# Small float32 matmuls of an attention stage moved into 64x32 and 128x32 tiles of TensorE, in a fused attention and two-MLP kernel

## The chip, the cores and the metric

The kernel is one program on one core of a Trainium2 chip. TensorE (PE in the rows; PEld is its weight loading, which runs beside the matmuls), VectorE (DVE), ScalarE (ACT) and SyncE (SP) take part; GpSimd only builds an identity matrix at the start. SP issues all DMAs. The metric is the device time of one execution in microseconds (us); the kernel before took 736.26 us, the median of three runs from 735.78 to 737.3.

## The reference

For each of 4 batches b and 8 heads h, tokens x[b,h] (512 x 64) and states st[b,h] (32 x 64) attend to each other, and two MLPs follow on all 4 x 544 rows:

```python
scores = scale * x @ state.T                 # 512 x 32 for each (b, h)
a = softmax(scores, over the 32 states)
xread = a @ state                            # 512 x 64
scores2 = scale * state @ x.T                # 32 x 512: the same products, transposed
a2 = softmax(scores2, over the 512 tokens)
sread = a2 @ x                               # 32 x 64
x = concat([xread, sread], axis=2)           # heads side by side: 2176 rows of 512
x = softplus(x @ w_in) @ w_out               # first MLP, d_ff 2048
h = x @ w_in2
out = (max(h, 0) + alpha * min(h, 0)) @ w_out2
```

All arrays are float32. The MLP products are made of three passes over "hi" and "lo" parts in a reduced float32 format; the scores and the states' read are plain float32 matmuls.

## The kernel before, in words

The weights arrive as 64-bit words that hold float32 numbers in another encoding; `decode` (L319) loads a chunk of 128 x 512 into a staging buffer and takes two ACT and two DVE operations to turn it into floats, and `split` (L252) makes the hi part on ACT and the lo part on DVE.

Attention of one batch has five parts. `scores` (L434) is called for two halves k of the 512 tokens. Each half is 8 matmuls whose stationary operand is a 128 x 128 block of x and whose moving operand is 64 columns of the states, zero-padded so that two heads share the 128 rows; the result stands with tokens in the partitions and (head, state) in the columns. ACT copies it to SBUF (L449), and DVE and ACT make the softmax over the 32 states of each head (L450 to L457). `columns` (L460) transposes that result for the first MLP. `rows` (L472) transposes the copied scores on TensorE (L478), so that (head, state) stands in the partitions, and takes the softmax over 512 tokens (L487 to L492). `back` (L502) transposes it again (L510). `read` (L515) multiplies: for each of 4 head pairs and 4 token blocks a 128 x 128 block of x is stationary and 64 columns of the softmax move (L523).

The first MLP uses that xread is a product too: instead of multiplying xread with w_in, `heads_of_m` (L543) multiplies the states with w_in head by head, in two row tiles of 64 partitions that lie side by side (L550), ACT copies the result to `tf` (L556), and `make_m` (L558) brings the four pieces of a batch together by DMA into `mf` and splits them into `m`. The first of these, for batch 0 and the first quarter of the columns, is made on TensorE by `make_first_m` (L573) with full 128 x 128 blocks of padded states (L580). A unit of the first MLP, `step1` (L612), is 6 matmuls `ph<-at,m`, a softplus on ACT (L586), a split into `gs`, and 12 matmuls `pa<-gs,wo` two units later. There are 64 units, 16 for each batch. The banks `ph` are two, so a unit can't begin before the softplus of the unit two before it has read its bank.

The order on each engine is set by a planner. A string (PROGRAM, L1064) lists the steps; each adds operations with engine, cost and dependencies to a graph (`G.add`), and `order` (L111) lists them by due time with a model of the engines. Where it sees TensorE idle near the start it puts in filler matmuls (L1056), each a 128 x 128 matmul on the identity, which write a bank that nobody reads. Each engine then runs its list strictly in that order, and SP issues its DMAs in order too.

The exponential and the softplus live in two different tables of ACT, and each change between them is an ACT_TABLE_LOAD.

Of the kernel before, what the change touches and what calls it, by code (L numbers as in the profile page):

```python
# [22 lines left out]
P = 128  # L23
# [10 lines left out]
NST = 2  # L34
# [39 lines left out]
class Graph:  # L74
# [36 lines left out]
    def order(self):  # L111
# [29 lines left out]
        while placed < n:  # L141
# [31 lines left out]
            if delay:  # L173
                busy = max(busy, t + LAND) + delay - LAND
                delay = busy - t - c
# [20 lines left out]
def attention_then_mlps_kernel(ctx: ExitStack, tc: tile.TileContext, xT, xn, st, st0, w1i, w1o, w2i, w2o, alpha, out):  # L196
# [31 lines left out]
    SB = [lambda b=b: part("sbb", None, F32, 1024)[:, b * 512:(b + 1) * 512] for b in range(2)]  # L228
    WO = [[part(f"wo{j}_{i}", None, F32R) for j in range(2)] for i in range(2)]
    STG = [part(f"st{i}", None, I64, 512) for i in range(NST)]  # L230
# [40 lines left out]
    def load(dst, src, w, r=(), nbytes=0):  # L271
        G.add(SP, 0.06, lambda: nc.sync.dma_start(out=now(dst), in_=now(src)), r, w, delay=LAND + nbytes / RATE)
# [39 lines left out]
    def stg(i):  # L312
        return STG[i] if i < NST else part("sbb", "stg2", I64, 512)

    def third_stage():
        G.add(SP, 0.0, lambda: None, [], [("sb", 0), ("sb", 1)] + [("st", NST, k) for k in range(4)])
        stages[1] = NST + 1

# [66 lines left out]
    def load_state(pair):  # L385
        load(stf, st[pair], [("xf", B)], nbytes=P * 2048)

    def state_of(b):
        return SB[b]().rearrange("p (c f) -> p c f", c=KC) if b < 2 else stf

    def load_first(b):
        load(lambda: SB[b]().rearrange("p (c f) -> p c f", c=KC), st0[b], [("sb", b)], nbytes=P * 2048)

# [12 lines left out]
    def attention(b):  # L406
# [4 lines left out]
        ssb = sz_t[:, :1024].rearrange("p (k c) -> p k c", k=4)  # L411
# [22 lines left out]
        def scores(k):  # L434
            p, pk = bank()
            p_s = p.rearrange("p (q c) -> p q c", q=2)

            def mm():
                for q in range(2):
                    for hp in range(4):  # L440
                        pos, half = hp ^ (b % 2), (hp ^ b) % 2
# [5 lines left out]
            sa, za = [szk[0]] if k == 0 else [szk[1]], [szk[2]] if k == 0 else [szk[3]]  # L447
            G.add(PE, 16 * NARROW, mm, xtk[2 * k:2 * k + 2] + [("sb", b) if b < 2 else ("xf", B)], [pk], load=0.24)
            G.add(ACT, act_us(512, True), lambda: A.activation(ssb[:, sk, :], p_s, AF.Copy), [pk], sa)  # L449
# [22 lines left out]
        def rows():  # L472
            ps = [bank() for _ in range(2)]

            def mm():
                for hg in range(2):
                    for blk in range(4):
                        T.transpose(ps[hg][0][:, blk * P:(blk + 1) * P], ssb[:, blk, hg * P:(hg + 1) * P], ident)  # L478

            G.add(PE, 0.88, mm, szk[:2], [ps[0][1], ps[1][1]], load=0.49)  # L480
            for hg in range(2):
                c = slice(hg, hg + 1)
                p, pk = ps[hg]
                nk, sk, ek = smk(("n", hg)), smk(("s", hg)), [szk[hg]]

                def chain(c=c, p=p, hg=hg):
                    return [lambda: V.tensor_reduce(out=nb[:, c], in_=p, axis=AX.X, op=ALU.max),  # L487
                            lambda: V.tensor_scalar(out=nb[:, c], in0=nb[:, c], scalar1=-SCALE, scalar2=None, op0=ALU.mult),
                            lambda: A.activation(e2[:, hg, :], p, AF.Exp, bias=nb[:, c], scale=SCALE, accum_out=s2[:, c]),
                            lambda: V.tensor_scalar(out=s2[:, c], in0=s2[:, c], scalar1=1e-9, scalar2=None, op0=ALU.add),  # L490
                            lambda: V.reciprocal(out=s2[:, c], in_=s2[:, c]),
                            lambda: V.tensor_scalar(out=e2[:, hg, :], in0=e2[:, hg, :], scalar1=s2[:, c], scalar2=None, op0=ALU.mult)]  # L492

                f = chain()
                G.add(DVE, dve_us(512), f[0], [pk], nk)
                G.add(DVE, 0.07, f[1], [], nk)
                G.add(ACT, 0.66, f[2], nk + [pk], ek + sk, table="exp")
                G.add(DVE, 0.07, f[3], [], sk)
                G.add(DVE, 0.07, f[4], [], sk)
                G.add(DVE, 0.4, f[5], sk, ek)  # L500
# [14 lines left out]
        def read():  # L515
            p, pk = bank(False)
            p_r = p[:, :256].rearrange("p (c f) -> p c f", c=KC)

            def mm():
                for hp in range(4):  # L520
# [5 lines left out]
            G.add(PE, 32 * NARROW, mm, xsk + szk[2:], [pk], load=0.24)  # L526
            cs = slice(b * NS, (b + 1) * NS)
            for j in range(2):
                pr = slice(64 * j, 64 * j + 64)
                half = j ^ (b >> 1)  # L530
                split(srt[pr, 0, :, cs], srt[pr, 1, :, cs], p_r[pr, :, half * NS:(half + 1) * NS], 128, [pk], [("sr", b, j)], psum=True)

        return {"l": lambda: (load_x(0), load_x(1), load_s()), "i": lambda: load_x(0), "j": lambda: load_x(1), "k": load_s,
                "s": lambda: (scores(0), scores(1)), "c": columns, "r": rows, "b": back, "x": read}
# [8 lines left out]
    def heads_of_m(g, c):  # L543
# [9 lines left out]
        for e in range(2):  # L553
            k = 2 * (c % 2) + e
            dst = TF[:, (4 * (c // 2) + k) * 512:(4 * (c // 2) + k + 1) * 512]
            G.add(ACT, act_us(512, True), lambda dst=dst, i=banks[e]: A.activation(dst, PX[i], AF.Copy), [("px", banks[e])], [("tf", c // 2, k)])  # L556

    def make_m(b, g):  # L558
# [5 lines left out]
        tf = TF.rearrange("p (h k f) -> p h k f", h=2, k=4)  # L564
        for q in range(4):
            k = q ^ (2 * (b & 1) + (b >> 1))
            r = slice(32 * q, 32 * q + 32)
            load(mf[r], tf[r, :, k, :], [("mf", i, hg, q) for hg in range(2)], [("tf", hg, k) for hg in range(2)], nbytes=32 * 4096)
# [4 lines left out]
    def make_first_m():  # L573
        s = mslot[0, 0] = ring("m", NM)
        for hg in range(2):
            i = ring("ph", 2)
            p, pk = PH[i], ("ph", i)
            for k in range(2):
                c = 2 * hg + k
                G.add(PE, 0.86, lambda p=p, c=c, k=k: T.matmul(p, state_of(0)[:, c, :], wf(c), start=k == 0, stop=k == 1),  # L580
                      [("sb", 0), ("wi", 1, c, "hi")], [pk])
            split(lambda hg=hg: m_ap(s)[:, 0, hg, :], lambda hg=hg: m_ap(s)[:, 1, hg, :], p, 512, [pk], [("m", s, hg, 0), ("m", s, hg, 1)], psum=True)
# [125 lines left out]
    XS = [("wi0_0", wik(0, 0)), ("wi1_0", wik(0, 1)), ("wo0_0", wok(0, 0)), ("wo1_0", wok(0, 1)), ("at0", atk(0)), ("tf", [("tf", hg, k) for hg in range(2) for k in range(4)]),  # L708
# [390 lines left out]
```

## Time and profile before

| | |
|---|---|
| median of 3 runs | 736.26 us (735.78 to 737.3) |
| profiled execution, own time | 736.82 us |
| its span, first to last instruction | 734.9 us |
| mean granted clock of TensorE | 0.995 of full |
| PE, PEld, DVE, ACT busy | 98%, 84%, 68%, 60% of the span |

A time in a row is counted from the start of the span. "a<-b" means that the instruction writes a and reads b. A plain float32 matmul leaves two records (x counts) for each instruction, and a transpose, or a matmul in the reduced format, one.

### The profile page before, as it was taken

To read this page: it belongs to the slowest core of one execution; us is meant where nothing else is said; L and a number is where in the kernel's file an instruction comes from. 1 tells how busy PE (TensorE), PEld (TensorE's weight loads), DVE (VectorE), ACT (ScalarE), POOL (GpSimd) and SP (SyncE) were. 2 spreads that over 40 slices of the span, in tenths; PEclk is the share of its full clock that TensorE was granted. 3 is DMA by queue.
4 is the path that set the end of the run, shared out by engine and by line. 5 is a ranking of instruction groups with operands and counts; after the bars stand their busy time and mean duration, and the time that the engine had idled before them with its cause. 6 is when DMAs were issued, how large, how long until landed. Compare 5 with 4: busy or idle time off the path is not lost.

```text
span 734.9 us, 10324 instructions
## 1 busy us (share of the span) xinstructions
PE 722.5 (98%) x3644; PEld 616.5 (84%) x3644; DVE 496.1 (68%) x935; ACT 438.9 (60%) x863; POOL 0.7 (0%) x6
## 2 busy tenths in 40 slices
PE   9998999999999999999999999999999999999996
PEld 8967887887788778888899988898898988888884
DVE  5978883776688678777889757954655664555452
ACT  5888986886776676776467545533444543443341
POOL 0000000000000000000000000000000000000000
PEclk9999999999999999999999999999999999999998
DMA  8559355574657588586569955455755454675632
GB/s 287 217 174 249 97 182 143 161 211 148 208 174 230 168 253 221 178 283 233 158 220 316 337 191 194 157 181 207 254 192 187 169 197 177 237 276 175 243 115 72
DMA packets 51224, 148.28 MB, mean 202 GB/s; under 512 B 7140, under 2 KB 21732, under 8 KB 44516
## 3 DMA queue, kind: packets, MB, share of 16 engines
q1 hardware_dynamic: 51172, 147.62, 61.0%
q8 instruction: 29, 0.48, 0.3%
q14 instruction: 23, 0.19, 0.1%
HBM read 112.21 MB, written 27.53 MB: 190 GB/s over the span
## 4 chain that ended last, share of the span: by engine, by line
PE 91%; ACT 4%; DVE 3%; issue 1%; DMA 1%; POOLq 0%; POOL 0%; ACTq 0%; DVEq 0%
PE pa L264 40%; PE ph L264 35%; PE px L264 9%; PE px L550 2%; PE px L523 1%; PE pa L1055 1%; DMA xf<-in_xn 1%; PE px L442 0%; PE pa L442 0%; PE pa L1056 0%; ACT tmp L586 0%; PE px L510 0%; ACT L586 0%; PE px L466 0%; DVE n_wo L895 0%
## 5 line engine op out<-in xcount | busy, mean ns | idle before, releaser
L264 PE MATMUL pa<-gs,wo 128*128 128x512 f32 x768 | 188.6, 394 | 1.1 <-ACT wo L254 0.9
L264 PEld LDWEIGHTS pa<-gs,wo 128*128 128x128 f32 x768 | 142.3, 188 | 34.6 <-issue 3.3
L886 ACT ACTIVATE n_gs<-n_gs 128x384 f32<-128x384 f32 (+1 forms) x96 | 48.6, 506 | 109.5 <-DVE tmp L888 72.3
L264 PE MATMUL ph<-at,m 128*128 128x512 f32 x384 | 98.7, 398 | 2.5 <-ACT tmp L586 2.4
L264 PEld LDWEIGHTS ph<-at,m 128*128 128x128 f32 x384 | 71.4, 189 | 20.0 <-ACT tmp L586 3.6
L264 PE MATMUL pa<-n_m,n_wo 128*128 128x512 f32 x288 | 78.0, 393 | 0.0
L264 PEld LDWEIGHTS pa<-n_m,n_wo 128*128 128x128 f32 x288 | 53.0, 188 | 8.2
L255 DVE TENSOR_TENSOR gs<-tmp,gs 128x512 fp32r<-128x512 f32 x64 | 43.9, 688 | 20.4 <-PE pa L264 16.8
L254 ACT ACTIVATE gs<-tmp 128x512 fp32r<-128x512 f32 x64 | 40.2, 630 | 24.1 <-PE pa L264 22.6
L586 ACT ACTIVATE tmp<-ph 128x512 f32<-128x512 f32 x68 | 40.1, 594 | 22.4 <-PE ph L264 16.4
L946 DVE TENSOR_TENSOR n_gs<-ph,n_z 128x384 f32<-128x384 f32 (+1 forms) x72 | 36.2, 524 | 24.9 <-PE ph L264 22.4
L330 DVE SCALAR_TENSOR_TENSOR st<-st 128x512 uint32<-128x512 uint32 x45 | 31.0, 690 | 30.3 <-ACT st L329 30.0
L888 DVE SCALAR_TENSOR_TENSOR tmp<-n_st,nalpha,n_gs 128x384 f32<-128x384 f32 (+1 forms) x72 | 42.4, 588 | 8.8 <-ACT n_st L887 7.0
L264 PE MATMUL pa<-n_at,n_m 128*128 128x512 f32 x144 | 40.0, 392 | 0.0
L264 PE MATMUL pa<-n_at,n_at 128*128 128x512 f32 x144 | 39.7, 393 | 0.0
L946 DVE TENSOR_TENSOR n_z<-ph,n_z 128x384 f32<-128x384 f32 (+1 forms) x36 | 18.9, 526 | 30.4 <-PE ph L264 30.2
L895 DVE TENSOR_TENSOR n_wo<-tmp,n_wo 128x384 fp32r<-128x384 f32 (+1 forms) x48 | 25.5, 532 | 20.5 <-ACT n_wo L893 15.1
L893 ACT ACTIVATE n_wo<-tmp 128x384 fp32r<-128x384 f32 (+1 forms) x48 | 23.8, 502 | 24.4 <-PE pa L264 10.4
L264 PE MATMUL ph<-n_wi,n_wi 128*128 128x384 f32 (+1 forms) x192 | 37.1, 329 | 0.1
L264 PE MATMUL ph<-n_wo,n_wi 128*128 128x384 f32 (+1 forms) x186 | 35.6, 328 | 0.0
L264 PEld LDWEIGHTS ph<-n_wi,n_wi 128*128 128x128 f32 x192 | 33.0, 188 | 2.8 <-DVE n_gs L946 0.6
L887 ACT ACTIVATE n_st<-n_gs 128x384 f32<-128x384 f32 (+1 forms) x72 | 34.9, 485 | 0.0
(232 smaller groups left out, 1261.4 us busy)
## 6 DMA issues: line engine op xcount, KB each, us to landing
n_wi<-w2i SPq DMA_DIRECT2D x16, 1024.0 KB, 5.5
w2i<-z SPq DMA_DIRECT2D x56, 256.0 KB, 3.6
st<-in_moe_w_in SPq DMA_DIRECT2D x25, 512.0 KB, 4.7
n_wi<-w2i SPq DMA_DIRECT2D x16, 768.0 KB, 5.1
n_at<-w2o SPq DMA_DIRECT2D x12, 1024.0 KB, 4.8
n_m<-w2o SPq DMA_DIRECT2D x12, 1024.0 KB, 4.8
st<-in_moe_w_out SPq DMA_DIRECT2D x20, 512.0 KB, 4.4
w2o<-z SPq DMA_DIRECT2D x32, 256.0 KB, 4.1
```

Source lines behind the costliest of these rows:

```text
L254: G.add(ACT, act_us(n, psum), lambda: A.activation(now(hi), now(src), AF.Copy), r, k + [x for x in also if x not in k])
L255: G.add(DVE, dve_us(n), lambda: V.tensor_tensor(out=now(lo), in0=now(src), in1=now(hi), op=ALU.subtract), list(r) + k, [x + ("lo",) for x ...
L264: T.matmul(acc, lhs[x], rhs[y], start=first and (x, y) == (0, 0), stop=last and len(part) - 1 == k and len(part) != 2)
L330: G.add(DVE, dve_us(512), lambda: V.scalar_tensor_tensor(out=words()[:, :, 0], in0=words()[:, :, 1], scalar=0x80000000, in1=words()[:, :, ...
L550: T.matmul(PX[banks[e]], stm[r, x, c, :], wi_ap(g, y)[r, c, :], start=k == 0, stop=k == 2)
L586: G.add(ACT, act_us(512, True), lambda: A.activation(TMP[i], h, AF.Softplus), [hk], [("tmp", i)], table="softplus")
L886: G.add(ACT, act_us(nt, psum), lambda: A.activation(cut(r), now(h), AF.Relu), [hk] + ro + list(own), [rk])
L887: G.add(ACT, act_us(nt, psum), lambda: A.activation(cut(m), now(h), AF.Relu, scale=-1.0), [hk] + mo + list(own), [mk])
L888: G.add(DVE, dve_us(nt), lambda: V.scalar_tensor_tensor(out=cut(g), in0=cut(m), scalar=nalpha[:, c:c + 1], in1=cut(r), op0=ALU.mult, op1=A ...
L893: G.add(ACT, act_us(nt, False), lambda: A.activation(hi()[:, sl], cut(g), AF.Copy), [gk, own1], [key + ("hi",)] + ([k for k in both(*[("f" ...
L895: G.add(DVE, dve_us(nt), lambda: V.tensor_tensor(out=lo()[:, sl], in0=cut(g), in1=hi()[:, sl], op=ALU.subtract), [gk, own1, key + ("hi",)] ...
L946: G.add(DVE, dve_us(nt), lambda: V.tensor_tensor(out=dst()[:, :nt], in0=h, in1=z()[:, :nt], op=ALU.add), [hk, zk] + own, [dk])
```

## The change

Five things are done in one step.

1. All states are loaded once, as a 128 x 512 block without padding (`load_state`, one DMA in the place of four), and `state_of(b, c, e)` is a 64 x 32 block of it.
2. `scores` makes the states stationary: 8 matmuls for a batch, each in its own 64 x 32 tile of the array (row half e, column quarter c), and each with 512 columns of x moving. The result stands with (head, state) in the partitions. ACT copies it (two copies, as before), and the softmax over the tokens now reads that copy. What used to be transposed for the rows is now transposed for the columns (`normalize`, 8 transposes for a batch, as many as before). `make_first_m` uses the same tiles.
3. `read` makes 32 columns of the softmax stationary in 128 x 32 tiles, with 64 columns of x moving: 32 matmuls for a batch in the place of 16. The division by the sum of the exponentials moves from the 512 wide rows to the 64 wide result (two DVE operations on 128 x 64), and the result is transposed once more (4 transposes in all) and split in one piece in the place of two.
4. The third staging buffer is there from the start and not from the second batch on.
5. `tf` has another layout, the planner's DMA costs are a little different, and PROGRAM is another string.

```diff
-NST = 2
+NST = 3
-    def load_state(pair):
-        load(stf, st[pair], [("xf", B)], nbytes=P * 2048)
+    def load_state():
+        load(stf, st, [("xf", B)], nbytes=P * 2048)
+    def state_of(b, c, e):
+        return stf[64 * e:64 * e + 64, c, 32 * (b ^ c):32 * (b ^ c) + 32]
...
-                        T.matmul(p_s[:, q, pos * 64:(pos + 1) * 64], xt(k)[:, hp, q * P:(q + 1) * P],
-                                 state_of(b)[:, hp, half * 64:(half + 1) * 64], start=True, stop=True)
+                for c in range(KC):
+                    for e in range(2):
+                        T.matmul(ps[e][0][32 * c:32 * c + 32, :].rearrange("p (k s) -> p k s", k=2), state_of(b, c, e), xa[64 * e:64 * e + 64, :, c, :],
+                                 start=True, stop=True)
+            for e in range(2):
+                G.add(ACT, act_us(512, True), lambda e=e: A.activation(e2[:, e, :], ps[e][0], AF.Copy), [ps[e][1]], [szk[e]])
...
+            def tr():
+                for q in range(2):
+                    for e in range(2):
+                        T.transpose(p_s[:, q, e * P:(e + 1) * P], e2[:, e, (2 * k + q) * P:(2 * k + q + 1) * P], ident)
...
-                            lambda: V.tensor_scalar(out=e2[:, hg, :], in0=e2[:, hg, :], scalar1=s2[:, c], scalar2=None, op0=ALU.mult)]
...
-                for hp in range(4):
-                    pos = hp ^ (b % 2)
+                for e in range(2):
                     for blk in range(4):
-                        T.matmul(p_r[:, hp, :], xs()[:, blk, hp * P:(hp + 1) * P], z[:, blk, pos * 64:(pos + 1) * 64],
-                                 start=(blk == 0), stop=(blk == 3))
+                        for c in range(KC):
+                            T.matmul(p_r[32 * c:32 * c + 32, 64 * e:64 * e + 64], z[:, blk, e * P + 32 * c:e * P + 32 * c + 32],
+                                     xs()[:, blk, (2 * c + e) * 64:(2 * c + e) * 64 + 64], start=(blk == 0), stop=(blk == 3))
...
+            G.add(PE, 0.12, lambda: T.transpose(t[:, :P], row, ident), [szk[0], szk[0] + (1,)], [tk], load=0.49)
...
-                      [("sb", 0), ("wi", 1, c, "hi")], [pk])
+                for e in range(2):
+                    T.matmul(PH[ps[e]][32 * c:32 * c + 32, :], state_of(0, c, e), wf(c)[64 * e:64 * e + 64], start=True, stop=True)
```

The order of the instructions moves on every engine. At the end of the first batch's attention, TensorE's list before the change, from the transposes for the rows to the first unit of the first MLP (L466 are the transposes for the columns, L510 those back, L1056 the fillers):

```order
L478 MATMUL pa_101<-ident,x2t_65 128x128 x4
L478 MATMUL pa_99<-ident,x2t_65 128x128 x4
L580 MATMUL ph_96<-wf,sbb 128x512
L1056 MATMUL pa_102<-ident 128x128 x15
L466 MATMUL pa_100<-ident,x2t_65 128x128 x4
L466 MATMUL pa_101<-ident,x2t_65 128x128 x4
L510 MATMUL px_97<-ident,x2t_65 128x128 x4
L510 MATMUL px_98<-ident,x2t_65 128x128 x4
L1056 MATMUL pa_102<-ident 128x128 x2
L442 MATMUL px_97<-sbb,xf_67 128x64 x8
L264 MATMUL ph_95<-at_288,m_217 128x512 x6
```

And the same place after it, where L451 are the transposes of `normalize`, L470 those for the columns and L1048 the fillers:

```order
L451 MATMUL pa_101<-ident,x2t_65 128x128 x4
L451 MATMUL pa_99<-ident,x2t_65 128x128 x4
L1048 MATMUL pa_102<-ident 128x128 x27
L470 MATMUL pa_100<-ident,x2t_65 128x128 x4
L470 MATMUL pa_101<-ident,x2t_65 128x128 x4
L1048 MATMUL pa_102<-ident 128x128 x13
L263 MATMUL ph_95<-at_317,m_247 128x512 x6
L432 MATMUL px_97<-xf_67,xf_69 32x512
```

The transposes back and half of the next batch's scores have moved behind the first unit, and 40 fillers stand here in the place of 17. At the program's start TensorE's list before is this (L1055 are the 16 matmuls that warm the engine up):

```order
L1055 MATMUL pa_102<-ident 128x128 x16
L1056 MATMUL pa_102<-ident 128x128 x12
L580 MATMUL ph_95<-wf,sbb 128x512
L1056 MATMUL pa_102<-ident 128x128 x3
L442 MATMUL pa_99<-sbb,xt_124 128x64 x8
```

After it:

```order
L1047 MATMUL pa_102<-ident 128x128 x16
L1048 MATMUL pa_102<-ident 128x128 x24
L546 MATMUL px_97<-wi_0_169,stm 128x512
L546 MATMUL px_98<-wi_0_169,stm 128x512
L546 MATMUL px_97<-wi_0_169,stm 128x512
L546 MATMUL px_98<-wi_0_169,stm 128x512
L546 MATMUL px_97<-wi_0_178,stm 128x512
L546 MATMUL px_98<-wi_0_178,stm 128x512
L1048 MATMUL pa_102<-ident 128x128 x5
L432 MATMUL pa_99<-xt_116,xf_69 32x512
```

The first product of states and w_in now comes ahead of the first scores, and 29 fillers stand here in the place of 15. In all there are 69 fillers after the change and 32 before it.

On ACT the exponentials of the two softmaxes move together. Before, around the third batch's softmax over the tokens (L489 its exponentials, L586 the softplus; those over the states, L453, stand some twenty rows ahead):

```order
L489 ACT_TABLE_LOAD
L489 ACTIVATE xf_67,small_93<-px_97,small_93 128x512
L489 ACTIVATE xf_67,small_93<-px_98,small_93 128x512
L374 ACTIVATE z_84<-st_79 128x2x128
L586 ACT_TABLE_LOAD
L586 ACTIVATE tmp_83<-ph_95 128x512
```

After, where L484 are the exponentials over the tokens, L457 those over the states and L582 the softplus:

```order
L484 ACT_TABLE_LOAD
L484 ACTIVATE xf_67,small_93<-xf_67,small_93 128x512
L457 ACTIVATE xf_67<-xf_67 128x512 x2
L484 ACTIVATE xf_67,small_93<-xf_67,small_93 128x512
L582 ACT_TABLE_LOAD
L582 ACTIVATE tmp_82<-ph_96 128x512
```

Both softmaxes of a batch now share one change of the table. Over the whole program ACT's list has 8 table loads in the place of 10.

## Rows read from the trace of the kernel before

**Rows 1.** The page, part 1: busy us, share of the span, instructions.
```profile
PE 722.5 (98%) x3644; PEld 616.5 (84%) x3644; DVE 496.1 (68%) x935; ACT 438.9 (60%) x863; POOL 0.7 (0%) x6
```

**Rows 2.** Busy time of each engine in stretches of 10 us.
```profile
core 0: us, PE busy (x) PEld busy (x) DVE busy (x) ACT busy (x) POOL busy (x), PEclk, DMA share, GB/s
...
20.00:30.00 10.00, 10.00 (x82) 9.37 (x81) 9.87 (x26) 7.99 (x16) 0.00 (x0) 1.00 0.79 310
30.00:40.00 10.00, 9.87 (x69) 8.80 (x69) 8.83 (x19) 9.89 (x17) 0.00 (x0) 1.00 0.50 162
40.00:50.00 10.00, 8.88 (x43) 6.19 (x43) 9.17 (x22) 9.97 (x20) 0.00 (x0) 1.00 0.35 111
50.00:60.00 10.00, 10.00 (x71) 8.28 (x72) 4.43 (x7) 7.14 (x14) 0.00 (x0) 1.00 0.91 242
60.00:70.00 10.00, 8.21 (x49) 6.57 (x48) 8.86 (x18) 8.99 (x18) 0.00 (x0) 1.00 0.90 271
70.00:80.00 10.00, 9.39 (x42) 7.96 (x43) 9.64 (x20) 10.00 (x19) 0.00 (x0) 0.83 0.70 212
80.00:90.00 10.00, 10.00 (x63) 8.80 (x63) 6.65 (x17) 9.77 (x19) 0.00 (x0) 1.00 0.09 32
```

**Rows 3.** Waits of PE: total us, times, longest us.
```profile
PE ph L264 <- ACT tmp L586: 2.4, 1, 2.4
PE pa L1055 <- POOL ident masks.py:199: 1.4, 1, 1.4
PE pa L264 <- ACT wo L254: 0.9, 1, 0.9
PE pa L264 <- DVE wo L255: 0.2, 1, 0.2
```

**Rows 4.** The chain that ended last, pieces: start us, us, what.
```profile
7.77 2.68 PE pa L1056 x24
...
13.71 1.77 PE ph L580 x4
...
55.98 3.53 PE px L523 x32
...
94.11 3.52 PE px L442 x32
...
100.67 0.87 PE px L478 x8
...
172.55 1.39 PE ph L264 x6
173.94 0.90 PE px L550 x6
```

**Rows 5.** PEld and PE in the second batch's read, from the timeline.
```profile
55.59 3.77 PEld L523 LDWEIGHTS px<-xf,xf 128*128 128x128 f32 x32
...
55.82 3.68 PE L523 MATMUL px<-xf,xf 128*128 128x64 f32 x32
```

**Rows 6.** The timeline: PE's first unit, then ACT and PE around 70 us.
```profile
27.69 1.64 PE L264 MATMUL ph<-at,m 128*128 128x512 f32 x6
...
68.67 1.28 ACT L586 ACT_TABLE_LOAD   x1
...
69.96 0.60 ACT L586 ACTIVATE tmp<-ph 128x512 f32<-128x512 f32 x1
...
70.61 2.06 PE L264 MATMUL ph<-at,m 128*128 128x512 f32 x6 [2.40 <-ACT tmp L586]
```

**Rows 7.** The stretch of low clock, columns as in rows 2.
```profile
71.80:75.10 3.30, 3.30 (x14) 2.81 (x13) 3.20 (x7) 3.30 (x7) 0.00 (x0) 0.51 0.78 251
```

**Rows 8.** ACT alone in two stretches: us, busy (instructions), PEclk, DMA share, GB/s.
```profile
30.00:50.00 20.00, 19.86 (x35) 1.00 0.42 136
...
58.00:90.00 32.00, 29.72 (x55) 0.95 0.59 173
```

More of the change, by code (lines that the diff above doesn't have):

```diff
@@ L173, in order @@
             if delay:
-                busy = max(busy, t + LAND) + delay - LAND
+                busy = max(busy, t + LAND) + c + delay - LAND
                 delay = busy - t - c
@@ L195, in attention_then_mlps_kernel @@
 @with_exitstack
-def attention_then_mlps_kernel(ctx: ExitStack, tc: tile.TileContext, xT, xn, st, st0, w1i, w1o, w2i, w2o, alpha, out):
+def attention_then_mlps_kernel(ctx: ExitStack, tc: tile.TileContext, xT, xn, st, w1i, w1o, w2i, w2o, alpha, out):
     nc = tc.nc
@@ L269, in steps, with load @@
         return [(PAIRS[:2], k) for k in range(n)] + [(PAIRS[2:], k) for k in range(n)]
-    def load(dst, src, w, r=(), nbytes=0):
-        G.add(SP, 0.06, lambda: nc.sync.dma_start(out=now(dst), in_=now(src)), r, w, delay=LAND + nbytes / RATE)
+    def load(dst, src, w, r=(), nbytes=0, cost=0.34):
+        G.add(SP, cost, lambda: nc.sync.dma_start(out=now(dst), in_=now(src)), r, w, delay=LAND - cost + nbytes / RATE)
     def wi_ap(g, j):
@@ L312, in stg @@
     def stg(i):
[L313 to L317, printed above, removed]
+        return STG[i] if i < NST - 1 else part("sbb", "stg2", I64, 512)
     def decode(src, extra=None, whole=None):
@@ L516, in read @@
             p, pk = bank(False)
-            p_r = p[:, :256].rearrange("p (c f) -> p c f", c=KC)
+            p_r = p[:, :P]
+            row = sz_t[:, :P]
             def mm():
-                for hp in range(4):
-                    pos = hp ^ (b % 2)
+                for e in range(2):
                     for blk in range(4):
-                        T.matmul(p_r[:, hp, :], xs()[:, blk, hp * P:(hp + 1) * P], z[:, blk, pos * 64:(pos + 1) * 64],
-                                 start=(blk == 0), stop=(blk == 3))
-            G.add(PE, 32 * NARROW, mm, xsk + szk[2:], [pk], load=0.24)
+                        for c in range(KC):
+                            T.matmul(p_r[32 * c:32 * c + 32, 64 * e:64 * e + 64], z[:, blk, e * P + 32 * c:e * P + 32 * c + 32],
+                                     xs()[:, blk, (2 * c + e) * 64:(2 * c + e) * 64 + 64], start=(blk == 0), stop=(blk == 3))
+            G.add(PE, 2.4, mm, xsk + szk[2:], [pk], load=0.24)
+            for e in range(2):
+                G.add(DVE, dve_us(64), lambda e=e: V.tensor_scalar(out=row[:, 64 * e:64 * e + 64], in0=p_r[:, 64 * e:64 * e + 64], scalar1=s2[:, e:e + 1],
+                                                                   scalar2=None, op0=ALU.mult), [pk] + smk(("s", e)), [szk[0] + (e,)] if e else [szk[0]])
+            t, tk = bank(False)
+            G.add(PE, 0.12, lambda: T.transpose(t[:, :P], row, ident), [szk[0], szk[0] + (1,)], [tk], load=0.49)
             cs = slice(b * NS, (b + 1) * NS)
[L528 to L531, printed above, removed]
+            split(srt[:, 0, :, cs], srt[:, 1, :, cs], t[:, :P].rearrange("p (c n) -> p c n", c=KC), 128, [tk], [("sr", b, 0), ("sr", b, 1)], psum=True)
         return {"l": lambda: (load_x(0), load_x(1), load_s()), "i": lambda: load_x(0), "j": lambda: load_x(1), "k": load_s,
-                "s": lambda: (scores(0), scores(1)), "c": columns, "r": rows, "b": back, "x": read}
+                "s": scores, "c": columns, "r": rows, "b": back, "x": read}
     mslot = {}
@@ L563, in make_m @@
         mf = MF[i].rearrange("p (h f) -> p h f", h=2)
[L564 to L568, printed above, removed]
+        tf = TF.rearrange("p (c h f) -> p c h f", c=KC, h=2)
+        for c in range(KC):
+            q = b ^ c
+            load(mf[32 * c:32 * c + 32], tf[32 * q:32 * q + 32, c], [("mf", i, hg, c) for hg in range(2)], [("tf", c, hg) for hg in range(2)], nbytes=32 * 4096, cost=0.6)
         for hg in range(2):
```

97 lines of the change are left out of this document (36 added, 61 removed).

## The prediction

> **What bounds the kernel now.** I read the page's busy times first: PE is busy for 98% of the span, DVE for 68%, ACT for 60% [rows 1]. So what PE is relieved of counts, wherever it is not given back as a wait. Then the stretches of 10 us: between 30 and 50 us ACT is busy almost without a gap, DVE for about nine tenths, and PE is not full; between 60 and 80 us it is the same, and the granted clock falls once [rows 2, 8]. From 80 us on PE is full. The waits of PE are few: 2.4 us on a softplus, 0.9 and 0.2 us on a split of w_out, 1.4 us at the start [rows 3]. The early stage is therefore one in which PE and ACT are both nearly the bound, and PE's share there is padded: 32 fillers stand in its list where the planner saw a wait. A filler is two records, and 24 records take 2.68 us [rows 4], so each filler is 0.223 us of PE that does nothing.
>
> The wait of 2.4 us ends with the softplus at 69.96 us, which itself stood behind a table load of 1.28 us [rows 6]. Behind it follows a stretch of 3.3 us at a granted clock of 0.51, that is near 1.2 GHz [rows 7]; it costs 3.3 x 0.49 = 1.6 us. With the waits of 2.4, 0.9 and 0.2 us, 5.1 us are lost between 40 and 76 us.
>
> **What is removed.** Scores: 16 matmuls for a batch take 3.52 us [rows 4], four batches 14.1 us. Read: 16 matmuls take 3.53 us, four batches 14.1 us. First m: two of its four matmuls take 1.77 us, all four 3.5 us. Together 31.7 us. All of it lies on PE, and the chain runs through it.
>
> **What is added.** Scores and first m are five groups of 8 matmuls, each with 512 moving columns. One full float32 matmul of 512 columns takes 1.77 / 2 = 0.885 us [rows 4]. The only tiles in the trace are the two row halves of L550: 6 matmuls take 0.90 us, where 6 untiled ones take 1.39 us [rows 4]. Three pairs at 1.39 / 6 = 0.23 us are 0.69 us, so two row tiles do run side by side, and 0.21 us goes to getting in and out of the tiles. That column tiles run side by side too, no row shows. The bounds of a group are 0.885 + 0.21 = 1.1 us, if all 8 do, and 8 x 0.885 = 7.1 us, if none do; 4 x 0.885 + 0.21 = 3.75 us, if only the row halves do. I take 1.2 us: the row halves behave as separate arrays, each matmul has a tile of its own here, and 0.1 us is for the start of eight in turn. Five groups are 6.0 us.
>
> The Trainium skill has a figure for this: "TensorE: Matmul & The Clock Gate", Part 3 on packing small matmuls, gives the span of a pack as one matmul and about 4 ns for each further tile, measured with column tiles too. By it a group would be an estimated 0.885 + 7 x 0.004 = 0.91 us and the five 1.4 us less than I take; no run here shows a column tile yet.
>
> A read is 32 matmuls, thus 64 records, with 64 moving columns and a load of 32 columns. Before, load and matmul go at the same pace, 3.77 and 3.68 us for 32 records [rows 5], that is 0.11 us for a load of 128 columns along the chain; the moving part would take only 64 / 512 x 0.885 / 2 = 0.055 us for a record. So the old read is bound by its loads. Loads of a quarter of the columns make 64 x 0.0276 = 1.8 us, with the change of tiles 2.0 us. The moving part is 64 x 0.055 = 3.5 us if it isn't overlapped and 0.9 us over four column tiles. The bounds are 0.9 + 0.21 = 1.1 us and, with 0.11 us for each record as now, 7.1 us. I take 2.4 us, near the pace of the loads and with something for the issue of twice as many instructions: four reads are 9.6 us. The four transposes at 0.87 / 8 [rows 4] are 0.4 us. The transposes for the columns, the rows and the way back are as many as before.
>
> So 6.0 + 9.6 + 0.4 = 16.0 us come for 31.7 us: PE does 15.7 us less work. But the list has 69 fillers in the place of 32: 37 x 0.223 = 8.3 us are given back. **Net 7.4 us.**
>
> **Is that time real?** Up to the first unit PE loses 24 old score matmuls (5.3 us), the first m (3.5 us) and the transposes back (0.9 us), and gains two groups (2.4 us) and all the fillers (8.3 us): the first unit comes 1.0 us later than its 27.69 us [rows 6], with more of the attention still behind it. Up to the fifth unit, the first of the second batch, PE's list before has 48 score matmuls, two reads and the first m (21.2 us); the new one has three groups, two reads, two transposes and the fillers (16.9 us), and three matmuls `pa<-gs` (0.7 us) that used to come later: it is 3.6 us shorter. ACT must follow. Its list ahead of the fifth softplus has 85 activations and 4 table loads, before 89 and 6. At 29.72 / 55 = 0.54 us each [rows 8] and 1.28 us for a load that is 4.7 us less. So both engines reach that place 3.6 to 4.7 us earlier, and the wait there is not enlarged. The table load that stood ahead of the softplus at 69.96 us is gone from that place, since the exponentials of both softmaxes now share one change of table. I count 1.2 us of the 2.4 us wait as gone, and, as the clock may then hold or not, half of its 1.6 us: 2.0 us. DVE has, for a batch, two operations of 512 columns less and two of 64 more, and one split in the place of two: a small relief. The three DMAs fewer and the early third buffer are hidden by the fillers ahead of the first products; if they aren't, what they are worth lies within the 5.1 us of stalls, as gain. The alpha load, which now stands second on SP's queue, delays the weights queued behind it by less than the 5.4 us that the 24 first fillers cover, so I cost it at nothing; were the cover gone it would show as a wait of PE at its first product.
>
> 7.4 + 2.0 = 9.4 us off the profiled execution's own 736.82 us is 727.4 us. That execution was 0.56 us above the median, so **727 us**. Its own range takes the groups at 1.1 to 1.5 us (0.5 less to 1.5 more), the reads at 2.0 to 3.5 us (1.6 less to 4.4 more), and of the stalls all or nothing back (3.1 less to 2.0 more): 722 to 733 us.
>
> **Rivals.** *Column tiles wait for each other.* A group then takes 3.75 us and a read 3.75 us: 5 x 2.55 + 4 x 1.35 = 18.2 us more than I take, 745 us, slower than before. For it: no row shows a column tile at work, and four streams of moving columns must enter the same rows of the array at once. Against it: the row halves overlap fully. It makes the kernel slower once five times a group's excess and four times a read's pass 9.4 us. I give it 9%.
>
> *The reads are bound by the number of instructions.* The closest that a load and its matmul follow each other anywhere in the rows is 0.11 us, for the transposes as for the old scores and reads [rows 4]. Half of that, 0.055 us, would be 3.5 + 0.2 us for a read: 5.3 us more, 732 us. At the full 0.11 us it would be 7.1 us, 18.8 us more and 746 us. Against it: in each of these rows a load of 128 columns is the other half of the pair, so they show no bound on the instruction itself. 15%. The Trainium skill, "TensorE: Matmul & The Clock Gate", step 2 of what happens when a matmul is issued, tells of about 62 ns for each matmul where the sequencer decodes in software; by that a read would be an estimated 4.0 us, longer than before, and the kernel about 733 us. The trace bears it out as little as it excludes it.
>
> *The new start slips.* The softmax over the states now waits for both copies on ACT and for transposes, where DVE read the scores from their bank before. The fillers cover that as planned; but they are spent whatever happens, so each us that the chain is longer than planned comes on top. Two copies at ACT's 0.54 us, the transposes' 0.9 us and a second stretch of low clock (1.6 us) are 3.6 us, and with the stalls' 2.0 us not gained it is 732.5 us. For it: ACT and DVE are as full as that from 30 us on [rows 2]. 12%.
>
> **Chances.** The forecast has 64%, the rivals 9, 15 and 12%. A measurement of this kernel can tell about 0.2%, 1.5 us, from no change. Faster by more: nearly all of the forecast and of the third rival, most of the second, 83%; within 0.2%: 5%; slower: the first rival and the far end of the second, 12%. For the range I let go of the first rival, the far end of the second and a little at the lower end: 721 to 736 us.
>
> **What would show it.** Right: L432 with 16 records in about 1.2 us and L517 with 64 in about 2.4 us on the chain; the fillers 138 records in some 15 us; the first unit near 28.7 us; 8 table loads on ACT; PE's waits and low clock between 40 and 80 us below 5 us. Wrong: a group of L432 over 3 us, a read over 3.5 us, a wait of PE ahead of the first product or behind the scores, or PE waiting longer for the softplus of the second batch than now.

## The result, and the profile after

The kernel after took 725.17 us, the median of four executions from 723.67 to 725.4, beside 736.78 us for the kernel before in the same comparison: a ratio of 0.9836 with a 95% interval of 0.9813 to 0.9859. That is 11.6 us less, where 727 us, 9.4 us less, were forecast. The profiled execution of after took 725.4 us; its span is 723.4 us and its mean granted clock 0.993. Two later executions, one of e1 (789.52 us, mean granted clock 0.851) and one of e5 (876.53 us, 0.753), fell in a slower state and are left out of every time below.

The page's first part of after, as in [rows 1]: busy us, share of the span, instructions.

```profile
PE 710.9 (98%) x3794; PEld 599.9 (83%) x3794; DVE 494.1 (68%) x931; ACT 434.7 (60%) x857; POOL 0.7 (0%) x6
```

PE is busy for 11.6 us less, 722.5 before against 710.9, and its idle time has not changed: 734.9 - 722.5 = 12.4 us before, 723.4 - 710.9 = 12.5 us after. So the gain shows as PE time and not as fewer gaps. Fillers count as busy here, though, and they grow (below): without them PE's work fell by 20.0 us, from 722.5 - 7.8 = 714.7 to 710.9 - 16.2 = 694.7 us, and 8.4 us of that stand in the list as filled waits. The new pieces on the chain of after (start us, us, what), to be held against [rows 4]:

```profile
64.10 1.02 PE px L432 x16
...
80.93 1.03 PE px L517 x64
```

A batch's scores went from 3.52 to 1.02 us and its read from 3.53 to 1.03 us; the last batch's are as long (1.02 us from 87.82 us, 1.03 us from 106.73 us). The groups of lines of after, fillers (L1048) and ACT's table loads (busy us, mean ns | idle before), and the fillers of before (L1056) in the same view:

```profile
L1048 PE MATMUL pa<-ident 128*128 128x128 f32 x138 | 16.2, 276 | 0.0
...
L582 ACT ACT_TABLE_LOAD x4 | 5.1, 1283 | 0.1
L484 ACT ACT_TABLE_LOAD x3 | 3.8, 1283 | 0.1
...
L245 ACT ACT_TABLE_LOAD x1 | 1.3, 1283 | 0.7 <-PEq L1076 0.7
```

```profile
L1056 PE MATMUL pa<-ident 128*128 128x128 f32 x64 | 7.8, 275 | 0.0
```

The fillers take 16.2 - 7.8 = 8.4 us more, where 8.3 us were forecast, and there are 8 table loads, as forecast. The waits of PE (total us, times, longest us) are other ones than in [rows 3]:

```profile
PE pa L1047 <- POOL ident masks.py:199: 1.4, 1, 1.4
PE px L517 <- ACT tf L551: 1.2, 1, 1.2
PE px L525 <- DVE xf L522: 1.2, 1, 1.2
PE px L546 <- ACT x2t L506: 0.5, 1, 0.5
PE ph L263 <- DVE n_gs L942: 0.4, 2, 0.3
PE pa L263 <- ACT gs L253: 0.2, 1, 0.2
PE pa L451 <- ACT x2t L437: 0.2, 1, 0.2
```

The 2.4 us on a softplus are gone, and so are those on w_out. In their place PE waits 1.2 us ahead of the first batch's read, 1.2 us ahead of the transpose of the second batch's read, and 0.9 us in three smaller ones. The last of them is a wait behind the scores. A stretch of 10 us, columns as in [rows 2], and below it the stretch of low clock that answers to [rows 7]:

```profile
40.00:50.00 10.00, 8.03 (x87) 5.86 (x86) 7.89 (x17) 9.97 (x18) 0.00 (x0) 0.70 0.42 101
...
44.00:50.60 6.60, 6.09 (x74) 4.94 (x75) 5.43 (x11) 6.57 (x12) 0.00 (x0) 0.50 0.52 135
```

The clock falls to half, 1.2 GHz, for 6.6 us, twice as long as before: 6.6 x 0.50 = 3.3 us lost, where it was 1.6 us. Before the fall PE has the waits of 0.5 and 1.2 us. That isn't the same in every execution: in a second profiled execution of the same kernel (c_after) the low clock begins only after the first read and lasts half as long.

```profile
47.05:50.30 3.25, 2.97 (x8) 2.31 (x9) 2.96 (x7) 3.22 (x6) 0.00 (x0) 0.50 0.79 212
```

The timeline of PE in after (start us, us, line, operation, [wait before it]) shows the first unit, the slow read, the first matmul `pa<-gs` behind it, the second wait and the fifth unit:

```profile
28.12 1.64 PE L263 MATMUL ph<-at,m 128*128 128x512 f32 x6
...
44.30 1.94 PE L517 MATMUL px<-xs,x2t 128*32 128x64 f32 x64 [1.21 <-ACT tf L551]
46.45 2.07 PE L263 MATMUL pa<-gs,wo 128*128 128x512 f32 x4 [0.21 <-ACT gs L253]
...
61.69 0.33 PE L525 MATMUL px<-ident,xf 128*128 128x128 f32 x1 [1.17 <-DVE xf L522]
...
62.56 1.54 PE L263 MATMUL ph<-at,m 128*128 128x512 f32 x6
```

In before the fifth unit stands here:

```profile
64.60 2.91 PE L264 MATMUL ph<-at,m 128*128 128x512 f32 x12
```

The first unit is 0.4 us later than in [rows 6], the fifth 2.0 us earlier, and the other 9.5 us come behind it, where two reads shrink, two batches' scores (2 x 1.02 us) stand in the place of one (3.52 us), and the wait of 2.4 us with its low clock stood. In c_after the first unit begins at 29.04 us, so that a difference of one us between single traces says little.

### The profile page after: what moved, and what is told of

Its sections match the earlier page's. It is cut to its first block, busy times and chain, and to the rows that moved or that the text cites. A ratio compares the mean times of both kernels' runs of the same rounds, so it can differ in the third digit from the quotient of the medians.

```text
span 723.4 us, 10597 instructions
## 1 busy us (share of the span) xinstructions
PE 710.9 (98%) x3794; PEld 599.9 (83%) x3794; DVE 494.1 (68%) x931; ACT 434.7 (60%) x857; POOL 0.7 (0%) x6
## 4 chain that ended last, share of the span: by engine, by line
PE 89%; DVE 5%; ACT 3%; DMA 1%; issue 1%; SPq 0%; DVEq 0%; ACTq 0%
PE pa L263 42%; PE ph L263 35%; PE px L263 9%; PE px L546 2%; DMA stg<-in_moe_w_in 1%; DVE n_gs L942 1%; DVE n_wo L891 0%; PE px L503 0%; DVE tmp L884 0%; PE px L470 0%; DVE small L482 0%; PE px L517 0%; PE px L432 0%; DVE wi L254 0%; ACT tf L551 0%
## 5 line engine op out<-in xcount | busy, mean ns | idle before, releaser
L263 PE MATMUL ph<-at,m 128*128 128x512 f32 x384 | 97.2, 396 | 0.0
L263 PEld LDWEIGHTS ph<-at,m 128*128 128x128 f32 x384 | 71.0, 188 | 18.3 <-issue 2.4
L582 ACT ACTIVATE tmp<-ph 128x512 f32<-128x512 f32 x68 | 40.4, 601 | 23.0 <-PE ph L263 20.7
L325 DVE SCALAR_TENSOR_TENSOR st<-st 128x512 uint32<-128x512 uint32 x45 | 31.1, 691 | 16.7 <-ACT st L324 16.2
```

Source lines behind the costliest of these rows:

```text
L263: T.matmul(acc, lhs[x], rhs[y], start=first and (x, y) == (0, 0), stop=last and len(part) - 1 == k and len(part) != 2)
L325: G.add(DVE, dve_us(512), lambda: V.scalar_tensor_tensor(out=words()[:, :, 0], in0=words()[:, :, 1], scalar=0x80000000, in1=words()[:, :, ...
L582: G.add(ACT, act_us(512, True), lambda: A.activation(TMP[i], h, AF.Softplus), [hk], [("tmp", i)], table="softplus")
```

## The experiments

The theory (A): what counts is PE's time; the tiled matmuls are short because four column tiles work at once; fillers only fill waits. The rivals: (B) much of the gain comes from the new order, the third buffer or the stalls; (C) the reads are short for another reason than the column tiles. Times are medians, and before took 736.7 to 737.2 us in the same comparisons.

**The read done three times** (e1).

```diff
-            G.add(PE, 2.4, mm, xsk + szk[2:], [pk], load=0.24)
+            G.add(PE, 2.4, lambda: [mm() for _ in range(3)], xsk + szk[2:], [pk], load=0.24)
```

> The 32 matmuls of each batch's read are issued three times over (the same sums, made anew each time), with the order of all other instructions unchanged; the output is the same. Measured for the changed kernel: one read 1.03 us, four of them in the first 110 us. Theory A (what PE saves in the attention stage is worth its full time at the end): 8 more reads x 1.03 = 8.2 us more, 733.4 us against 725.2. Theory B (the early stage is bound by ACT and DVE, so PE's saving there is only half real): the two reads before 60 us hide in PE's waits on ACT, the other two count: 4.1 us more, 729.3 us.

Measured: 732.93 us (732.69 to 733.13), a ratio of 0.9952 [0.9935, 0.9968], 7.8 us more than after for 8 more reads, 8 x 1.03 = 8.2 us. The total is theory A's, but its parts are not. The fifth unit, and the stretches of issue on the chain (PE waits for nothing that the profile shows), which after doesn't have there:

```profile
65.22 1.52 PE L263 MATMUL ph<-at,m 128*128 128x512 f32 x6
```

```profile
61.90 1.45 issue
...
85.62 0.42 issue
...
115.45 1.00 issue
```

The fifth unit comes 2.7 us later than in after (62.56 us), with four more reads, 4.1 us, ahead of it; 1.45 of the 2.7 us are issue. Behind it, four more reads and 1.4 us of issue make 7.8 - 2.7 = 5.1 us. So the late reads count nearly in full, and of the early ones a part is hidden, as theory B had it. With the 2.9 us of issue on top, theory A's 8.2 us would be 11.1 us and theory B's 4.1 us 7.0 us. On the other side the low clock lasts only about 3.4 us here, and the wait of 1.2 us at L525 is gone. That the total is so near 8.2 us is therefore luck in part, and it does not decide between the two.

**The read column by column** (e2): four matmuls in a row go to the same column tile, instead of to the four in turn.

```diff
                 for e in range(2):
-                    for blk in range(4):
-                        for c in range(KC):
+                    for c in range(KC):
+                        for blk in range(4):
```

> The loops of the read are exchanged, so that four matmuls in a row go to the same column tile of 32 and not to four different ones; the same matmuls, the same sums, everything else unchanged. Theory A (the read is short because neighbours lie in different column tiles and stream side by side): four in a row now stream one after the other, 64 records x 0.055 us = 3.5 us a read in the place of 1.03, 10 us more in all, 735 us. Theory B (the read is short because a record of 32 loaded and 64 moving columns is short in itself, 16 ns each): the read stays near 1.0 us and the time at 725 us.

Measured: 726.83 us, 0.9869 [0.9855, 0.9884]. On the chain of e2 a read takes 2.34 us:

```profile
56.78 2.34 PE px L517 x64
...
79.09 2.34 PE px L517 x64
```

So the order alone more than doubles it. The time of the kernel by itself would have spoken for theory B; the length of the read speaks for A. What has begun in the first 0.07 us of the second batch's read shows why, in after and then in e2; below them stand the first 0.1 us of a group of scores in after (start us, us, what):

```profile
58.53 0.26 PE L517 MATMUL px<-xf,xf 128*32 128x64 f32 x4
```

```profile
56.71 0.24 PE L517 MATMUL px<-xf,xf 128*32 128x64 f32 x1
```

```profile
29.69 0.66 PE L432 MATMUL px<-xf,xf 64*32 64x512 f32 x8
```

The starts of the single records in the two traces go on like this. In after four records begin together, 7 ns apart, as many as there are column tiles, and from the second four on a new four begins every 0.056 us: 16 x 0.056 = 0.89 us. In e2 the records begin one by one, also 0.056 us apart (the first two 0.08 us). That is the moving time of 0.055 us for a record in both, so in after four column tiles work at once. It isn't 64 x 0.055 = 3.5 us in e2, because there a second series, by the order of the matmuls that of the next column tile, begins after 0.25 us, when the first has four of its eight records behind it, and so on: two work at once. Why not more, no run shows. The group of scores begins in all eight tiles within 0.05 us.

Of the 4 x 1.31 = 5.2 us more in reads, 1.7 us reach the time. The waits ahead of the first read are those of after, but the clock held, and the wait at L525 is gone:

```profile
42.03 0.97 PE L546 MATMUL px<-wi,stm 64*128 64x512 f32 x5 [0.54 <-ACT x2t L506]
44.22 2.41 PE L517 MATMUL px<-xs,x2t 128*32 128x64 f32 x64 [1.22 <-ACT tf L551]
...
59.86 0.33 PE L525 MATMUL px<-ident,xf 128*128 128x128 f32 x1
...
60.73 1.54 PE L263 MATMUL ph<-at,m 128*128 128x512 f32 x6
```

```profile
40.00:50.00 10.00, 8.24 (x94) 6.01 (x94) 7.92 (x17) 9.97 (x19) 0.00 (x0) 1.00 0.47 123
```

So the waits alone don't bring the low clock. And the first two reads, 2.6 us longer together, cost nothing up to the fifth unit: it comes at 60.73 us, and at 60.80 us in e9 (below), whose clock held too and whose reads are short; the first units of the two are at 28.06 and 28.16 us. The whole span of e2 is 3.1 us longer than that of e9 (724.6 and 721.5 us), near the 2.6 us of the other two reads. By these two traces, shortening the early reads from 2.34 to 1.03 us is worth nothing, and shortening the late ones about its full length.

**No fillers** (e3).

```diff
-    G.filler = lambda: T.matmul(PA[3][:, :P], ident, ident, start=True, stop=True)
+    G.filler = lambda: None
```

> All 69 filler matmuls are left out (the 16 that warm PE up stay), the order of all other instructions unchanged; the output is the same. Theory A (the fillers stand where PE would wait anyway, for DVE and ACT in the first batch's attention): the first unit stays near 28 us, the time at 725 us, up to 3 us more if PE's clock is low there. Theory B (they are spent time, as the sum of the prediction had it: 8.3 us given back): the first unit comes some 5 to 15 us earlier and the kernel takes 717 us or less.

Measured: 725.49 us, 0.9851 [0.9834, 0.9868], no difference from after. PE is busy for 698.9 us, 12.0 us less, and the span is the same 723.4 us. Its waits, and its first unit:

```profile
PE pa L470 <- DVE x2t L461: 5.1, 1, 5.1
PE px L546 <- ACT stm L253: 4.9, 1, 4.9
```

```profile
27.29 3.20 PE L263 MATMUL ph<-at,m 128*128 128x512 f32 x6
```

```profile
10.00:20.00 10.00, 7.14 (x46) 3.16 (x46) 8.37 (x14) 8.43 (x16) 0.00 (x0) 0.50 1.02 419
```

The fillers stand in waits. Without them the first unit begins 0.8 us earlier, which is no more than after and c_after differ by, runs at half clock and takes 3.20 in the place of 1.64 us.

**The tiles with the old order** (e4): the string of before with the one load of states put first.

```diff
-PROGRAM = "w0 n w0 w0 t0 w0 F v0 w0 p0 i0 j0 s0 h00
...
+PROGRAM = "t0 w0 w0 w0 v0 i0 w0 w0 j0 l1 F w0 v0 v0 s0 n p0 r0 w0 c0 h00
...
```

> The string of steps of the kernel before, with the load of the states put first and the steps that no longer exist left out, and all else as in the changed kernel; the output is the same. The planner then puts in 82 fillers in the place of 69 and 6 table loads of ACT in the place of 8. Theory A (the tiles are what makes the kernel faster, the new string only lets it show): between the two kernels and nearer to the changed one, 727 to 730 us, 2 to 5 us more for 13 fillers and later units. Theory B (the new order is what makes it faster): 735 us or more, as before the change.

Measured: 728.63 us, 0.9894 [0.9879, 0.9909]. With the old string the other parts (tiles, the early third buffer, the one load of states) bring 736.7 - 728.6 = 8.1 us; the new string brings 3.5 us. PE's list then holds 98 fillers, of two records each, and not the 82 expected:

```profile
L1048 PE MATMUL pa<-ident 128*128 128x128 f32 x196 | 24.4, 278 | 0.0
```

**The two waits ahead of the first read filled** (e5, and e9, the same kernel again beside after): six matmuls on the identity ahead of the first batch's read, four within the `heads_of_m` that waits for its bank.

```diff
-            G.add(PE, 2.4, mm, xsk + szk[2:], [pk], load=0.24)
+            G.add(PE, 2.4, (lambda: ([T.matmul(PH[0][:, :P], ident, ident, start=True, stop=True) for _ in range(6)], mm())) if b == 0 else mm, xsk + szk[2:], [pk], load=0.24)
...
+                    if nth == 2 and (k, e) == (0, 0):
+                        [T.matmul(PH[0][:, :P], ident, ident, start=True, stop=True) for _ in range(4)]
```

> In the changed kernel's list two waits of PE at 41.6 and 43.1 us are filled: 4 matmuls on the identity after the first matmul of the third product of states and w_in, and 6 ahead of the first read, into a bank that is free there; 2.2 us of work for 2.2 us of waits, all else unchanged, the output the same. Theory A (those waits bring the granted clock to 0.50 from 44 to 50.6 us, which costs 3.3 us): the clock stays up and the kernel takes 3 us less, 722 us. Theory B (the low clock costs nothing, since ACT is the bound up to 60 us and PE would wait for it anyway): 725 us as before, with longer waits of PE in the place of the low clock.

> The kernel of e5_gap_fill once more, beside the changed kernel on the same chip, since its profile fell in a disturbed run. Theory A (the two filled waits are what brings the clock to 0.50 for 6.6 us, at 3.3 us): the clock of 40 to 50 us is near 1.0, and the kernel is 2 to 3 us faster than the changed one. Theory B (ACT is the bound up to 62 us, and what the clock gives back PE waits for later): the clock is up, PE waits more at 55 to 62 us, and the kernel is 0 to 1.5 us faster.

> The changed kernel itself, to stand beside the others on the same chip: 725 us, clock 0.5 from 44 to 50.6 us if the profiled execution is like the first.

Measured: 724.0 us (0.982 [0.9807, 0.9833]) and 723.48 us (0.9822 [0.9809, 0.9836]); after beside e9 took 724.76 us, 0.9836 [0.9823, 0.985]. The intervals overlap, but the spreads tell more: nine executions of this kernel took 723.28 to 724.28 us, at a mean granted clock of 0.997 to 0.999; of eight of after, at 0.993 to 0.997, three lie there (723.67, 723.82, 724.03) and five at 725.05 to 725.53. A stretch of e9 as above, and its read, the `pa<-gs` behind it and its fifth unit:

```profile
44.00:50.60 6.60, 6.26 (x93) 4.48 (x93) 5.44 (x11) 6.57 (x13) 0.00 (x0) 1.00 0.62 156
```

```profile
45.02 1.10 PE L517 MATMUL px<-xs,x2t 128*32 128x64 f32 x64
46.45 1.19 PE L263 MATMUL pa<-gs,wo 128*128 128x512 f32 x4 [0.33 <-ACT gs L253]
...
60.80 1.54 PE L263 MATMUL ph<-at,m 128*128 128x512 f32 x6
```

The same places in c_after, whose clock was at 1.00 during the read and at 0.50 from 47.05 to 50.30 us (44 to 50.6 us had been expected):

```profile
47.33 2.08 PE L263 MATMUL pa<-gs,wo 128*128 128x512 f32 x4 [1.05 <-ACT gs L253]
...
62.86 1.54 PE L263 MATMUL ph<-at,m 128*128 128x512 f32 x6
```

With the waits filled, the clock stays at 1.00 in the profiled execution. What it gives back is less than theory A's 3.3 us. The `pa<-gs` behind the read waits for ACT in all three traces and begins 18.3 us after the first unit in each, whether the read ran at low clock (after) or at full clock, and with the waits filled or not; so what the low clock costs ahead of that place is hidden by ACT, as theory B had it. Behind it, after still has 4.2 us and c_after 3.0 us of low clock, half of which is 2.1 and 1.5 us. From first to fifth unit it is 34.4 us in after, 33.8 in c_after and 32.6 in e9: 1.8 and 1.2 us more than with the clock held, and 1.3 us is the difference of the medians of c_after and e9. This is the fastest version of all, by its median.

**No third buffer in the first stage** (e6), **and the third buffer only from the second batch on** (e8). In e6 the first edit stands alone, in e8 both do.

```diff
-    stages = [0, NST]
+    stages = [0, NST - 1]
...
+                if c == "s1":
+                    stages[1] = NST
```

> The changed kernel with two staging buffers from the start to the end of the first stage, in the place of three; the string of steps is the same, the planner then puts in 63 fillers in the place of 69, and they stand at more places; the output is the same. Theory A (the third buffer, early, is a small part of the gain): 725 to 727 us. Theory B (the third buffer is what lets the weights be ready ahead of the units): ACT waits for weights, PE for units, 729 us or more.

> The changed kernel with two staging buffers up to the second batch's scores and the third one from there on, as before the change (the kernel before had, beside these, room for two more chunks of the first quarter, this one for one); the string of steps is the same, the planner puts in 90 fillers in the place of 69; the output is the same. Theory A (the early third buffer is a small part of the gain; the 48 us that the kernel without any third buffer lost come from the later batches): 725 to 729 us. Theory B (the early third buffer carries the gain): 733 us or more.

Measured: e6 773.11 us, 1.0491 [1.0478, 1.0505]. It tells little of the change, because before had the buffer from the second batch on. Half of the loss of 48 us stands in three waits:

```profile
PE pa L263 <- ACT wo L253: 24.8, 3, 12.9
```

e8 undoes what the change did: 729.36 us, 0.9899 [0.9882, 0.9915], 4.6 us slower than after beside e9. Its first and its fifth unit, and its fillers:

```profile
30.66 1.67 PE L263 MATMUL ph<-at,m 128*128 128x512 f32 x6 [0.16 <-DVE m L254]
...
59.08 1.55 PE L263 MATMUL ph<-at,m 128*128 128x512 f32 x6
```

```profile
L1050 PE MATMUL pa<-ident 128*128 128x128 f32 x180 | 22.5, 279 | 0.0
```

The first unit comes 2.5 us later than in after (1.6 us later than in c_after), but the fifth 3.5 us earlier, so the loss isn't that of the first unit; it comes behind the fifth. The planner also puts in 90 fillers in the place of 69 and makes another list. So the early third buffer is worth some 4 us with this string and this planner; where they are lost without it, no run shows. What it is worth with the old string wasn't tried.

**The planner given the measured costs** (e7): reads 2.4 to 1.03, scores and first m 1.2 to 1.03, the DVE operations on 64 columns to 0.24 us.

```diff
-            G.add(PE, 2.4, mm, xsk + szk[2:], [pk], load=0.24)
+            G.add(PE, 1.03, mm, xsk + szk[2:], [pk], load=0.24)
...
-        G.add(PE, 1.2, mm, [("xf", B)] + [("wi", 1, c, "hi") for c in range(KC)], [("ph", i) for i in ps], load=0.7)
+        G.add(PE, 1.03, mm, [("xf", B)] + [("wi", 1, c, "hi") for c in range(KC)], [("ph", i) for i in ps], load=0.7)
```

> The planner's costs are set to what the changed kernel's trace shows: scores and first m 1.03 us in the place of 1.2, the read 1.03 in the place of 2.4, the two small divisions on DVE 0.24 in the place of 0.136; the string of steps is the same, the order of units and reads changes between 38 and 110 us; the output is the same. Theory A (the list waits where the planner's costs were wrong: 1.2 us each ahead of the first read and of its transpose): up to 3 us less, 722 to 725 us. Theory B (the order is robust, or the string was chosen for the old costs): 725 to 727 us.

Measured: 726.2 us, 0.9849 [0.9836, 0.9862], not faster than after. The list it makes has a new wait at its head:

```profile
PE px L503 <- DVE at L254: 2.2, 1, 2.2
```

Its profiled execution also has a granted clock of 0.74 from 40 to 50 us and 0.83 from 70 to 80 us. So the measured costs alone don't give a better list; what they would give with a string chosen for them wasn't tried.

## Why the prediction was right, and where its sum was not

| step | forecast, us | measured, us |
|---|---|---|
| removed from PE | 31.7 | 31.7 (the rows of before) |
| five groups of tiled matmuls | 6.0 | 5 x 1.02 = 5.1 |
| four reads | 9.6 | 4 x 1.03 = 4.1 at full clock |
| transposes of the read | 0.4 | 0.4 (taken as forecast) |
| fillers | 8.3 more | 8.4 more |
| waits gained | } 2.0 less | none (idle 12.4 and 12.5) |
| low clock | } | 1.7 more (3.3 against 1.6) |
| sum | 9.4 less | 12.0 less worked out, 11.5 less in the span |

**What is removed, and what bounds the kernel.** Right in the form in which it was put, that what PE is relieved of counts "wherever it is not given back as a wait". PE's tiled pieces are 31.7 - 9.6 = 22.1 us shorter, and about half of it reaches the time. 8.4 us are given back ahead of the first unit, as filled waits, and of the early reads' saving a part is given back too, in the new waits (e1, e2).

**The groups and the reads.** The read is the term that was mis-sized: 2.4 us taken, 1.03 us measured, 5.5 us in all; the groups add 0.9 us. I took the reads for bound by their loads, at a quarter of the old time each. They are not: four records begin together every 0.056 us, the moving time of one record, where four loads at a quarter of the old pace would take 0.11 us. The moving time is 64 records x 0.055 us over four column tiles, 0.885 us, as for a group, and both measure 0.14 us above it. Both also lie below the lower bound that I gave, 1.1 us, since the 0.21 us that I took from L550 for getting in and out of tiles is not paid here in full. By the Trainium skill, "TensorE: Matmul & The Clock Gate", Part 3 on packing small matmuls, a group was an estimated 0.91 us. The measured 1.02 us lie between that and my 1.2 us, nearer to the page.

**The fillers.** Their 8.3 us are there, and in the balance of PE's busy time the step holds. But e3 shows that they are no cost of their own: what stands behind them is the chain of decoding and softmaxes at the start, on DVE and ACT, and without them the same time is a wait. So the number that is given back is right, and its reason is the wait and not the fillers.

**Is that time real.** The first unit was forecast at 28.7 us and came at 28.12 us. For the fifth I argued that both engines reach it 3.6 to 4.7 us earlier; it came 2.0 us earlier. The wait on the softplus is gone altogether, as the moved table load let expect, and not only 1.2 us of it. But 2.0 us of stalls were to be won, and 1.7 us were lost: PE, with shorter reads than planned, now waits for the copy to `tf` (L551), where ACT is busy for 9.97 of 10 us, and for the division on DVE (L522) that the change put between a read and its transpose. I had counted this division as a relief of DVE by length, and not as a link between two steps of PE. The sign "PE's waits and low clock between 40 and 80 us below 5 us" did not come out: 0.5 + 1.2 + 0.2 + 1.2 us of waits and 3.3 us for the clock are 6.4 us. Of the signs of being wrong, a wait behind the scores came, of 0.2 us, and in c_after one ahead of the first product, of 0.45 us; both are too short to matter.

Two of the forecast's terms, 6.4 us too much on PE and 3.7 us too little in stalls, thus went against each other. That the time came out within 2 us of 727 us is to that extent luck. The prediction's own first range, 722 to 733 us, also ends too low by its terms: 1.5 + 4.4 + 2.0 = 7.9 us above 727 us is 735 us. The last range, 721 to 736 us, isn't touched by that.

**The third buffer.** I cost its early start at no more than the stalls. e8 puts 4.6 us on it, which is within those 5.1 us, but as the price of its loss in another list, not as a gain over before.

**The rivals.** *Column tiles wait for each other*: not borne out, 1.02 us and not 3.75 us for a group; e2 shows what a read costs when the same tile comes again and again, 2.34 us. *The reads are bound by the number of instructions*: not borne out, 64 records in 1.03 us are 16 ns each, far below the 55 ns that this rival took. The Trainium skill, "TensorE: Matmul & The Clock Gate", step 2 of what happens when a matmul is issued, gives about 62 ns for each matmul that is decoded in software; the estimate of 4.0 us counted each record as one, and with 32 matmuls it is 2.0 us. This trace has no such price: 1.03 us are 32 ns for each of the 32 matmuls. *The new start slips*: its first unit did not, 28.12 us, and the clock held at 1.00 around it; the longer stretch of low clock came at 44 us, behind other waits.

What stays open: what the tiles of the scores, those of the read and those of the first m are worth one by one, since no run took one of them alone; what the one load of states and the moved order are worth apart from each other inside the 3.5 us of the new string; why two executions of one kernel lose the clock for 6.6 and for 3.3 us, and e2, with the same two waits, not at all; and whether the wait of 1.2 us at L525 would give its time back, since e2 lost it together with the low clock.

## What to carry to other kernels

In this kernel a group of small matmuls took its moving columns divided by the column tiles in use, plus 0.14 us, with consecutive matmuls in different tiles; cost it so before its loads or its count. When a step on the fullest engine shrinks, look at the operation of another engine that stands between it and the next step: its latency, not its share of that engine, is the next wait. A total that fits isn't yet the mechanism: compare where single units begin, since time saved ahead of a place that waits for another engine is given back there. Fillers in a wait are not a loss to be counted on as gain; take them away once and see.

## What the runs showed of the hardware

- 64 records of float32 matmuls with 64 moving columns in 128 x 32 tiles take 1.03 us at full clock when four column tiles are used in turn (after), and 2.34 us when four matmuls in a row use one (e2). In after four records begin every 0.056 us; in e2 two series of records overlap, each with 0.056 us from one to the next.
- A group of 8 matmuls of 512 columns in 64 x 32 tiles takes 1.02 us (after), where one untiled matmul of 512 columns takes 0.885 us (before).
- Waits of 0.5 and 1.2 us preceded 6.6 us at a granted clock of 0.50 in after and 3.3 us in c_after, where it began within a third wait, of 1.05 us; in e2, with the same two waits, the clock stayed at 1.00, and so it did in e9, with 20 records of work on the identity in them.
